# Linear attention feeding a swish MLP on one core: seven half products for batch 1 too, and a new order of loads, casts and sums around it

## The chip, the cores and the metric

The kernel runs on one core of a Trainium2 chip. The metric is the device time of one execution in microseconds (us); the time of a kernel is the median over its runs. Times inside an execution come from one profiled run and count from the start of its span.

The engines are TensorE (PE in the profile; its weight loads are PEld), VectorE (DVE), ScalarE (ACT), GpSimd (POOL) and SyncE (SP, which here only issues DMAs).

## The reference

Inputs q, k, v have the shape 8 x 8 x 576 x 64 (batch, heads, sequence, head size), float32. With phi(x) = max(x, 0) + 1 for positive x and exp(x) otherwise:

```python
kv  = einsum('bhsd,bhse->bhde', phi(k), v)
z   = sum over s of phi(k)
num = einsum('bhsd,bhde->bhse', phi(q), kv)
den = einsum('bhsd,bhd->bhs', phi(q), z)[..., None] + 1e-06
x   = (num / den), heads side by side: 4608 tokens x 512
h   = x @ w_in                      # 512 x 2048
g   = h / (1 + exp(-beta * h))
out = g @ w_out                     # 2048 x 512, output 4608 x 512
```

## The kernel before

**Tiling.** A batch has 576 tokens: 512 of them are handled in the batch's own stages, and the last 64 of every batch are collected in `xT_tail` and handled together as a ninth piece of 512. Matmuls take bfloat16 and sum in float32 in PSUM. TensorE's program is therefore H0, Y0, H1, Y1, ..., H8, Y8. Hb computes h for 16 blocks of 128 hidden units (`h_phase`, four matmuls of 512 columns a block, L401) and ScalarE turns each block into g by a SiLU (L409). Yb multiplies g with w_out. Batch 0 has code of its own; the loop at the end of the kernel runs b = 1 to 8.

**Work for later batches lies between.** During Hb, `side` lists (`sh`, run after a given block; `sy`, run after a given product of Yb) insert: `kv_both(b+1)` (72 small matmuls, L223, and a copy to `kv_q`), `numer_all(b+1)` (72 small matmuls, L333; VectorE then divides and writes `xs_sb`, the evacuation, L346 to L348; SP transposes it into xT, L355, and its last 64 tokens into `xT_tail`, four transposes, L368), and during Yb the phi of batch b+2: per half an exponential on ScalarE (L163), a ReLU (L168) and a minimum (L175) on VectorE, and for q two DMA transposes to `qTd` (L273), which the numerators read.

**Loads.** `next_loads(b+1)` stands on GpSimd after block 0 of Hb: two casts of v (float32 `vf` to bfloat16 `vaug`, L241), a copy into `gate` (L856) that waits for `qTd` of b+1 and so holds back what follows, and then the loads of q, k and v of batch b+2, in this order, on GpSimd's queue.

**Two forms of Y.** `y_phase` (b = 1) takes 4 token tiles times 16 blocks of g, 64 matmuls of 512 columns (L416); VectorE copies each tile out. `y_fast` (b = 2 to 8, the tuple FAST) computes a 2 x 2 block product by seven half-size products (L792), 16 matmuls of 256 columns each: pa, pd, pa again, pc, pb, pd again, pb again. Four of its operands are sums of parts of g (`gs`, 8 x 256 a partition each, written by `g_diff` after blocks 3 and 7 and by `g_sums` after blocks 11 and 15 of Hb, L722 to L728), four are sums of parts of w_out (`ws`, L710, two in H1 after block 15, two in H2 after blocks 7 and 8). Between the products VectorE adds: u2 = pc + r1 and u3 = pd + u2 (L816, L817), then y parts from pb + u3 (L827), pd + u2 (L830), pb + u2 (L838). The second pd product needs u3 read from its bank first, the last pb product needs the add at L827.

**Order.** Every engine runs its own instructions in the order in which the code issues them (`manual_schedule`); waits are on semaphores. PSUM banks rotate among four single banks (`bank`) and two double ones (`banks`).

Of the kernel before, what the change touches and what calls it, by code (L numbers as in the profile page):

```python
# [9 lines left out]
BF16 = mybir.dt.bfloat16  # L10
# [6 lines left out]
def kernel(  # L17
# [21 lines left out]
    EA = D + 1  # L39
    HM = DM // 2  # L40
    TINY = 2.0 ** -30
    FAST = tuple(range(2, 9))

    ctx.enter_context(tc.manual_schedule())

# [21 lines left out]
    w_in_sb = [consts.tile([P, KC, 512], BF16, name=f"w_in{i}") for i in range(4)]  # L67
    w_out_sb = [consts.tile([P, 4, DM], BF16, name=f"w_out{i}") for i in range(4)]

    xT = [consts.tile([P, 2, 4, 2, P], BF16, name=f"xT{i}") for i in range(2)]  # L70
    xT_tail = consts.tile([P, KC, B * G], BF16, name="xT_tail")
    g_sb = [consts.tile([P, FC, 512], BF16, name=f"g{i}") for i in range(2)]
    stage = consts.tile([P, 4096], F32, name="stage")
    warm = consts.tile([P, 512], BF16, name="warm")
# [21 lines left out]
    ws = [consts.tile([P, 8, HM], BF16, name=f"ws{i}") for i in range(4)] if FAST else None  # L96


    def load(eng, dst, src, b, i0=0, n=4):
# [109 lines left out]
    def half(hh):  # L209
        return slice(hh * G, (hh + 1) * G)  # L210
# [108 lines left out]
    def numer_all(b):  # L319

        h = [bank("nps"), bank("nps")]
        w = [banks("nps") for _ in range(2)]
        for v in (*range(7, 14), *range(7), *range(14, 18)):
            t, a = v // 4, v % 2
            for il in range(2):
                ps = h[il] if v // 7 == 1 else w[v // 14][:, il]  # L330
                for n in range(2):
                    pr, j = (v % 4 // 2, 2 * t + n) if v < 16 else (n, J - 1)
                    nc.tensor.matmul(  # L333
                        ps[half(n), v % 7 * EA : (v % 7 + 1) * EA],
                        st[b, "qTd"][half(il), a, pr * J + j, :],
                        kv_q[b % 2][half(il), a, pr, :],
                        start=True, stop=True, skip_group_check=True,
                    )
# [13 lines left out]

        def trans(t):
            for il in range(2):
                nc.sync.dma_start_transpose(  # L355
                    out=xT[b % 2][:, il, t : t + 2].rearrange("p t r n -> p (t r) n"),
                    in_=xs_sb[:, il, t * 4 * D : (t + 2) * 4 * D],
                )

        for il in range(2):  # L360
            evac(h[il][:, None], slice(il, il + 1), 7, 14)
        evac(w[0], slice(0, 2), 0, 7)
        trans(0)
        evac(w[1], slice(0, 2), 14, 18)
        trans(2)
        for pr in range(2):
            for il in range(2):
                nc.sync.dma_start_transpose(  # L368
                    out=xT_tail[:, 2 * pr + il, b * G : (b + 1) * G],
                    in_=xs_sb[half(pr), il, 16 * D : 18 * D],  # L370
                )

    def x_dst(b, t):
        if t < NT - 1:
            return xT[b % 2][:, :, t].rearrange("p i r n -> p r i n")
        return xT_tail[:, :, b * G : (b + 1) * G].rearrange("p (r i) n -> p r i n", i=2)

    def x_trans(b, t, eng, tp=None):
        n = rows_of(t)
# [7 lines left out]
        copy(eng, x_dst(b, t), tp[:, :, :n].rearrange("p (r i) n -> p r i n", i=2))  # L387

    def x_trans_dma(b, t=NT - 1):
        nc.sync.dma_start_transpose(  # L390
            out=xT_tail[:, :, b * G : (b + 1) * G], in_=st[b, "xs", t][: rows_of(t)]
        )


    def h_mm(x, ff, hp, c0=0, c1=512):
        for kc in range(KC):
            if x is xT_tail:
                xm = x[:, kc, c0:c1].rearrange("p (t n) -> p t n", n=P)
            else:
                xm = x[:, kc % 2, c0 // P : c1 // P, kc // 2]  # L400
            nc.tensor.matmul(  # L401
                hp[:, c0:c1].rearrange("p (t n) -> p t n", n=P),
                w_in_sb[ff // 4][:, kc, (ff % 4) * P : (ff % 4 + 1) * P],
                xm,
                start=(kc == 0), stop=(kc == KC - 1), skip_group_check=True,
            )
# [55 lines left out]
    def load_v(b):  # L462
        if b < B:
            load(nc.gpsimd, vf, v, b)


    idle(11)
# [162 lines left out]
    for x in ("q", "k"):  # L630
        phi_tile(1, x)
        for pr in range(2):
            phi_exp(1, x, pr, xin(1, x, pr))
            phi_relu(1, x, pr, xin(1, x, pr))
    phi_min(1, "q", 0)
    phi_min(1, "q", 1)
    for i in range(2):
# [55 lines left out]
        y_store(0, t)  # L693
    phi_all(2, "k", exps=False)

    if FAST:

        def wq(i, c0):
            return w_out_sb[i][:, :, c0 : c0 + HM]

        def w_sum(k, n):

            r = slice(4 * n, 4 * n + 4)
            a, b = (
                (wq(n, HM), wq(n, 0)),
                (wq(2 + n, HM), ws[0][:, r]),
                (wq(2 + n, HM), wq(n, HM)),
                (wq(2 + n, 0), ws[1][:, r]),
            )[k]
            nc.vector.tensor_sub(ws[k][:, r], a, b)  # L710


    def run(side, n):
        for f in side.get(n, ()):
# [9 lines left out]
    def g_sums(b, c0, c1):  # L724
# [2 lines left out]
        nc.vector.tensor_sub(gs[1][:, c], gs[0][:, c], g[:, c, 0:HM])  # L727
        nc.vector.tensor_sub(gs[3][:, c], g[:, c2, 0:HM], gs[1][:, c])  # L728

    def h_phase(b, x, side):  # L730
        for ff in range(FC):
            if b == 1 and ff in (4, 5):

                if ff == 4:
                    pair = banks("h_ps")
                    for i in range(2):
                        h_mm(x, ff + i, pair[:, i])
                hp = pair[:, ff - 4]
            else:
                hp = bank("h_ps")  # L740
                h_mm(x, ff, hp)
            silu(b, ff, hp)
# [7 lines left out]
    def y_phase(b, side):  # L750
        last = b == B
        for t in range(4):
            yp = bank("y_ps")
            if last and t == 3:
                for c0, c1 in ((0, 320), (320, 512)):
                    for i in range(4):
                        y_mm(b, t, i, yp, c0, c1)
                    y_out(b, t, yp, c0, c1)
                break
            for i in range(4):  # L760
                y_mm(b, t, i, yp)
                if i < 3:
                    run(side, 4 * t + i)
            y_out(b, t, yp)
            run(side, 4 * t + 3)

    def y_fast(b, side):

# [17 lines left out]
        def wsum(n):  # L786
            return lambda c: ws[n][:, c, :]

        def product(ps, lhs, rhs, first, ts=range(2), apart=False):
            for p in ts:  # L790
                for c in range(8):
                    nc.tensor.matmul(  # L792
                        ps[:, p * HM : (p + 1) * HM], lhs(c, p), rhs(c),
                        start=(first and (p == 0 or apart) and c == 0), stop=True,
# [21 lines left out]
        nc.vector.tensor_add(u2, pc, r1)  # L816
        nc.vector.tensor_add(u3, pd, u2)  # L817
        run(side, 3)
# [31 lines left out]

    def next_loads(b):

        for pr in range(2):
            v_copy(nc.gpsimd, b, pr)
        if b + 1 < B:
            nc.gpsimd.tensor_copy(gate, st[b, "qTd"][:, 1, 2 * J - 1, G - 1 : G])  # L856
            load_qk(b + 1)
            load_v(b + 1)

    for b in range(1, B + 1):  # L860
        n, m = b + 1, b + 2
# [5 lines left out]
        if b in (1, 2) and FAST:  # L867
            for k_ in ((0, 2), (1, 3))[b - 1]:
                for n_ in range(2):
                    at(sh, 15 if b == 1 else 7 + k_ // 2, lambda k_=k_, n_=n_: w_sum(k_, n_))  # L870
        if m < B:
            y = (lambda a, f: f) if b in FAST else (lambda a, f: a)
            at(sy, 0, lambda: phi_tile(m, "q"), lambda: phi_part(m, "q", 0))
            at(sy, 1, lambda: phi_part(m, "q", 1))
            at(sy, 1, lambda: q_trans_dma(m))
            at(sy, y(6, 3), lambda: phi_tile(m, "k"), lambda: phi_part(m, "k", 0))
            at(sy, y(8, 4), lambda: phi_part(m, "k", 1), lambda: table(ACTF.Silu))
        h_phase(b, xT[b % 2] if b < B else xT_tail, sh)
        (y_fast if b in FAST else y_phase)(b, sy)


# [28 lines left out]
```

## Time and profile before

| | us |
|---|---|
| median of 3 runs | 278.6 |
| lowest and highest | 277.94 and 280.63 |
| the profiled execution | 279.42 |
| its span, first to last instruction | 277.6 |
| TensorE's chain, H1 begins, Y1 begins, H2 begins | 51.5, 67.03, 80.84 |
| Y2 begins, H3 begins, Y3 begins | 96.70, 110.66, 126.35 |
| loads of batch 3 issued on GpSimd: q, k, v | 62.05, 62.78, 63.52 |
| their times from issue to landing | 6.9, 9.3, 12.4 |
| loads of batch 4 issued: q, k, v | 87.02, 87.76, 88.49 |
| their times from issue to landing | 6.7, 12.8, 16.6 |

A timeline line gives the start, the busy time, the engine, the line of the kernel, the operation, the tiles (written <- read), the type, how many instructions are merged, and in brackets the idle time before it and what ended that. A window line gives, for a stretch of the span, the length and each engine's busy time. Lines of the waits give who waited for whom, the total, how often and the longest.

Where the change does its work, SP's queue reads in the old kernel as follows: four transposes of x, four of its last tokens, then q's two, and the stores of y behind them.

```profile
91.12 10.01 SPq L355 DMA_TRANSPOSE xT<-xs_sb  x4
101.18 7.08 SPq L368 DMA_TRANSPOSE xT_tail<-xs_sb  x4
108.42 3.45 SPq L273 DMA_TRANSPOSE qTd<-phi_q  x2
111.97 2.06 SPq L834 DMA_DIRECT2D out_dram<-y  x2
```

### The profile page before, as it was taken

The page shows a single profiled execution, that of the slowest core. Times are in us where ns is not written, and L with a number is a line of the kernel's source. Part 1 is how long each engine was busy: PE and PEld are TensorE (multiplying, and loading weights), DVE is VectorE, ACT ScalarE, POOL GpSimd, SP SyncE. Part 2 cuts the span into 40 slices and gives each one's busy share as a digit, 9 for nine tenths or more (in the row PEclk, how much of TensorE's full clock was granted, in tenths as well). Part 3 has the DMA queues.
Part 4 walks back from the last instruction along what each step waited for, and adds up shares of the span by engine and source line. Part 5 has one row for each costly group of instructions (what it writes and reads, how often), then busy time and mean ns, then how long its engine had stood idle before and what let it go on. Part 6 is the DMA issues. An engine that isn't in the chain of part 4 may idle for free.

```text
span 277.6 us, 6371 instructions
## 1 busy us (share of the span) xinstructions
PE 269.1 (97%) x2697; PEld 167.5 (60%) x2697; DVE 163.4 (59%) x311; ACT 170.1 (61%) x232; POOL 44.3 (16%) x60
## 2 busy tenths in 40 slices
PE   7899999999999997999999999999999999999994
PEld 2585455444444486548854885488548844874584
DVE  4861485967946869467746784679464413341432
ACT  5738897965915793578557855785573077217610
POOL 5922011042033003300330033030000000000000
PEclk9979999999999999999999999999999999999999
DMA  7999999569938994899789979985621050023013
GB/s 253 239 206 353 269 372 267 140 106 186 278 69 144 232 207 75 195 175 227 89 165 233 211 73 185 259 159 68 176 57 31 0 153 0 0 48 105 0 40 113
DMA packets 49612, 42.76 MB, mean 154 GB/s; under 512 B 31136, under 2 KB 41392, under 8 KB 49584
## 3 DMA queue, kind: packets, MB, share of 16 engines
q0 software_dynamic: 13040, 23.40, 36.9%
q1 hardware_dynamic: 36368, 18.82, 35.8%
q8 instruction: 21, 0.34, 0.6%
q10 hardware_dynamic: 176, 0.14, 0.2%
q14 instruction: 7, 0.06, 0.1%
HBM read 36.71 MB, written 9.44 MB: 166 GB/s over the span
## 4 chain that ended last, share of the span: by engine, by line
PE 66%; SPq 4%; DVE 2%; DMA 2%; issue 1%; DVEq 0%
PE h_ps L401 34%; PE ya L792 9%; PE yb L792 8%; PE yd L792 8%; PE yc L792 4%; SPq L368 2%; DMA qTd<-phi_q 2%; PE nps L333 1%; PE kvp L223 1%; SPq L355 1%; DVE r L168 1%; SPq L273 0%; DVE ws L710 0%; DVE u L816 0%; DVE u L817 0%
## 5 line engine op out<-in xcount | busy, mean ns | idle before, releaser
L409 ACT ACTIVATE g<-h_ps,beta_c 128x512 bf16<-128x512 f32 x144 | 97.7, 688 | 70.5 <-PE h_ps L401 70.5
L401 PE MATMUL h_ps<-xT,w_in 128*128 128x512 bf16 (+1 forms) x560 | 114.5, 361 | 0.0
L401 PEld LDWEIGHTS <-w_in 128*128 128x128 bf16 x624 | 57.3, 98 | 62.3
L792 PEld LDWEIGHTS <-stage 128*128 128x128 bf16 x448 | 43.8, 98 | 7.0 <-issue 1.7
L792 PEld LDWEIGHTS <-g 128*128 128x128 bf16 x336 | 32.8, 98 | 5.4
L241 POOL CAST vaug<-vf 128x1152 bf16<-128x1152 f32 x13 | 16.8, 1319 | 82.1 <-DMA vf<-in_v_dram 82.1
L416 PE MATMUL y_ps<-w_out,g 128*128 128x512 bf16 x128 | 29.1, 379 | 0.0
L792 PE MATMUL ya<-w_out,g 128*128 128x256 bf16 x224 | 26.7, 273 | 0.0
L722 DVE TENSOR_TENSOR stage<-g 128x1024 bf16<-128x1024 bf16 x14 | 9.6, 689 | 22.9 <-ACT g L409 22.9
L726 DVE TENSOR_TENSOR stage<-g 128x1024 bf16<-128x1024 bf16 x14 | 9.7, 691 | 22.6 <-ACT g L409 22.6
L416 PEld LDWEIGHTS <-g 128*128 128x128 bf16 x128 | 12.2, 98 | 13.5
L348 DVE TENSOR_TENSOR xs_sb<-nps,rden 128x448 bf16<-128x448 f32 (+2 forms) x24 | 18.2, 758 | 0.8
L163 ACT ACTIVATE e<-xk 128x1152 bf16<-128x1152 bf16 (+1 forms) x15 | 16.7, 1159 | 0.2 <-DMA xk<-in_k_dram 0.2
L163 ACT ACTIVATE e<-xq 128x1152 bf16<-128x1152 bf16 x14 | 15.6, 1159 | 0.0
L175 DVE TENSOR_TENSOR phi_k<-e,r 128x1152 bf16<-128x1152 bf16 x16 | 14.3, 897 | 1.7 <-DVE r L168 0.5
L175 DVE TENSOR_TENSOR phi_q<-e,r 128x1152 bf16<-128x1152 bf16 x16 | 13.0, 814 | 3.6 <-ACT e L163 2.7
L792 PE MATMUL yb<-w_out,stage 128*128 128x256 bf16 x112 | 13.4, 272 | 1.6 <-DVE y L827 1.6
L156 ACT ACT_TABLE_LOAD x11 | 14.1, 1283 | 0.2
L401 PE MATMUL h_ps<-xT_tail,w_in 128*128 128x512 bf16 x64 | 14.0, 379 | 0.0
L816 DVE TENSOR_TENSOR u<-yc,r 128x512 f32<-128x512 f32 x7 | 4.8, 690 | 15.4 <-PE yc L792 15.4
L792 PE MATMUL yb<-ws,stage 128*128 128x256 bf16 x112 | 13.4, 273 | 0.0
L792 PE MATMUL yc<-ws,stage 128*128 128x256 bf16 x112 | 13.4, 273 | 0.0
(98 smaller groups left out, 238.7 us busy)
## 6 DMA issues: line engine op xcount, KB each, us to landing
vf<-in_v_dram POOLq DMA_DIRECT2D x7, 1152.0 KB, 15.1
out_dram<-y SPq DMA_DIRECT2D x25, 256.0 KB, 3.8
xq<-in_q_dram POOLq DMA_DIRECT2D x7, 576.0 KB, 8.7
xk<-in_k_dram POOLq DMA_DIRECT2D x7, 576.0 KB, 12.8
out_dram<-y SPq DMA_DIRECT2D x17, 128.0 KB, 3.3
w_in<-in_moe_w_in_dram POOLq DMA_DIRECT2D x4, 512.0 KB, 11.3
g<-in_moe_w_out_dram POOLq DMA_DIRECT2D x2, 1024.0 KB, 17.1
stage<-in_moe_w_out_dram POOLq DMA_DIRECT2D x2, 1024.0 KB, 21.8
```

Source lines behind the costliest of these rows:

```text
L156: nc.scalar.activation(act0, warm[:, 0:1], func)
L163: nc.scalar.activation(e, x, ACTF.Exp)
L175: nc.vector.tensor_tensor(st[b, a][:, pr].rearrange("p j (h d) -> p j h d", h=2), st[b, a, pr, "e"].rearrange("p h j d -> p j h d"), st[b, ...
L241: eng.tensor_copy(dst, src)
L348: nc.vector.tensor_mul(xs_sb[:, ils, v0 * D : v1 * D].rearrange("p i (u d) -> p i u d", d=D), pv[:, :, :, 0:D], rden[:, :, :, None].to_bro ...
L368: nc.sync.dma_start_transpose(out=xT_tail[:, 2 * pr + il, b * G : (b + 1) * G], in_=xs_sb[half(pr), il, 16 * D : 18 * D],)
L401: nc.tensor.matmul(hp[:, c0:c1].rearrange("p (t n) -> p t n", n=P), w_in_sb[ff // 4][:, kc, (ff % 4) * P : (ff % 4 + 1) * P], xm, start=(k ...
L409: nc.scalar.activation(g_sb[b % 2][:, ff, :], hp, ACTF.Silu, scale=beta_c[:, ff : ff + 1])
L416: nc.tensor.matmul(yp[:, c0:c1], g_sb[b % 2][:, ff, t * P : (t + 1) * P], w_out_sb[i][:, c, c0:c1], start=(ff == 0), stop=(ff == FC - 1), ...
L722: nc.vector.tensor_sub(gs[2][:, c], g[:, c, 0:HM], g[:, c, HM:512])
L726: nc.vector.tensor_add(gs[0][:, c], g[:, c, HM:512], g[:, c2, HM:512])
L792: nc.tensor.matmul(ps[:, p * HM : (p + 1) * HM], lhs(c, p), rhs(c), start=(first and (p == 0 or apart) and c == 0), stop=True, skip_group_ ...
```

## The change

It has four parts.

1. FAST and `y_phase` go; `y_fast` serves batch 1 too. The w sums move: `w_sum(0)` into Y0 (between q's and k's ReLUs of batch 1), `w_sum(2)` after block 4 and `w_sum(1)` after block 9 of H1, `w_sum(3)` after the first product of Y1. In Y1 the product pc takes four blocks of g for both token halves and then the other four.
2. In H1, what stands in the side list of a block comes ahead of that block's g sums, and batch 2's numerators stand after block 11 in place of 12. In H2 kv stands after block 2 and the numerators after block 5 (before: 1 and 4). In Y1, phi of batch 3 is spread: q's two exponentials early, q's ReLU and minimum after the adds of u3 and after the next y add, k's after the next two.
3. `next_loads` loads v first, then q and k, and the two casts of v stand behind these loads, that is in Hb after landing. (Batch 2's casts stay ahead of the gate.)
4. The last x transposes take the odd 64 tokens along as a fifth block (`trans(8, 18)`), and the four tail transposes of a batch go; GpSimd copies the fifth block from xT to `xT_tail` (`tail_copy`, after block 0 of Hb, ahead of the gate, for b = 2 to 7). `xT` and `xT_tail` get other layouts for it. Batch 1's tail is transposed in two pieces in place of one.

```diff
-    FAST = tuple(range(2, 9))
...
-    xT = [consts.tile([P, 2, 4, 2, P], BF16, name=f"xT{i}") for i in range(2)]
-    xT_tail = consts.tile([P, KC, B * G], BF16, name="xT_tail")
+    xT = [consts.tile([P, 2, 9, P], BF16, name=f"xT{i}") for i in range(2)]
+    xT_tail = consts.tile([P, 2, B, 2, G], BF16, name="xT_tail")
...
-        trans(0)
+        trans(0, 8)
         evac(w[1], slice(0, 2), 14, 18)
-        trans(2)
-        for pr in range(2):
-            for il in range(2):
-                nc.sync.dma_start_transpose(
-                    out=xT_tail[:, 2 * pr + il, b * G : (b + 1) * G],
-                    in_=xs_sb[half(pr), il, 16 * D : 18 * D],
-                )
+        trans(8, 18)
+
+    def tail_copy(b):
+        nc.gpsimd.tensor_copy(
+            xT_tail[:, :, b].rearrange("p i r n -> p i (r n)"), xT[b % 2][:, :, 8]
+        )
...
+        if x == "q":
+            w_sum(0)
...
             silu(b, ff, hp)
-            if b in FAST:
-                if ff in (3, 7):
-                    g_diff(b, slice(ff - 3, ff + 1))
-                if ff in (11, 15):
-                    g_sums(b, ff - 11, ff - 7)
+            if b > 1:
+                g_parts(b, ff)
             run(side, ff)
+            if b == 1:
+                g_parts(b, ff)
...
-        product(pc, sums(1), wsum(1), True)
+        product(pc, sums(1), wsum(1), True, step=4 if b == 1 else 8)
...
-        for pr in range(2):
+        for pr in range(2) if b == 2 else ():
             v_copy(nc.gpsimd, b, pr)
         if b + 1 < B:
             nc.gpsimd.tensor_copy(gate, st[b, "qTd"][:, 1, 2 * J - 1, G - 1 : G])
+            load_v(b + 1)
             load_qk(b + 1)
-            load_v(b + 1)
+            for pr in range(2):
+                v_copy(nc.gpsimd, b + 1, pr)
...
+        if 2 <= b < B:
+            at(sh, 0, lambda: tail_copy(b))
         if n < B:
             at(sh, 0, lambda: next_loads(n))
-            at(sh, 9 if b == 1 else 1, lambda: kv_both(n))
-            at(sh, 12 if b == 1 else 4, lambda: numer_all(n))
+            at(sh, {1: 9, 2: 2}.get(b, 1), lambda: kv_both(n))
+            at(sh, {1: 11, 2: 5}.get(b, 4), lambda: numer_all(n))
+        if b == 1:
+            at(sh, 4, lambda: w_sum(2))
+            at(sh, 9, lambda: w_sum(1))
+            at(sy, 0, lambda: w_sum(3))
         if m < B:
...
+            at(sy, 0, lambda: phi_tile(m, "q"), lambda: phi_tile(m, "k"))
+            if b == 1:
+                for pr in range(2):
+                    at(sy, 0, lambda pr=pr: phi_exp(m, "q", pr, xin(m, "q", pr)))
+                    at(sy, 3 + pr, lambda pr=pr: phi_relu(m, "q", pr, xin(m, "q", pr)))
+                    at(sy, 3 + pr, lambda pr=pr: phi_min(m, "q", pr))
+                at(sy, 4, lambda: q_trans_dma(m))
+                at(sy, 5, lambda: phi_part(m, "k", 0))
+                at(sy, 6, lambda: phi_part(m, "k", 1), lambda: table(ACTF.Silu))
+            else:
...
-        (y_fast if b in FAST else y_phase)(b, sy)
+        y_fast(b, sy)
```

For b = 2 to 5 the phi steps stay after products 0, 1, 3 and 4, as in the old kernel.

More of the change, by code (lines that the diff above doesn't have):

```diff
@@ L95 @@
     ]
-    ws = [consts.tile([P, 8, HM], BF16, name=f"ws{i}") for i in range(4)] if FAST else None
+    ws = [consts.tile([P, 8, HM], BF16, name=f"ws{i}") for i in range(4)]
     def load(eng, dst, src, b, i0=0, n=4):
@@ L351, in evac, with trans @@
             )
-        def trans(t):
+        def trans(v0, v1):
             for il in range(2):
                 nc.sync.dma_start_transpose(
-                    out=xT[b % 2][:, il, t : t + 2].rearrange("p t r n -> p (t r) n"),
-                    in_=xs_sb[:, il, t * 4 * D : (t + 2) * 4 * D],
+                    out=xT[b % 2][:, il, v0 // 2 : v1 // 2],
+                    in_=xs_sb[:, il, v0 * D : v1 * D],
                 )
@@ L362, in numer_all @@
         evac(w[0], slice(0, 2), 0, 7)
-        trans(0)
+        trans(0, 8)
         evac(w[1], slice(0, 2), 14, 18)
-        trans(2)
-        for pr in range(2):
-            for il in range(2):
-                nc.sync.dma_start_transpose(
-                    out=xT_tail[:, 2 * pr + il, b * G : (b + 1) * G],
-                    in_=xs_sb[half(pr), il, 16 * D : 18 * D],
-                )
+        trans(8, 18)
[3 more added lines that the diff above has]
+        )
     def x_dst(b, t):
         if t < NT - 1:
-            return xT[b % 2][:, :, t].rearrange("p i r n -> p r i n")
-        return xT_tail[:, :, b * G : (b + 1) * G].rearrange("p (r i) n -> p r i n", i=2)
+            return xT[b % 2][:, :, 2 * t : 2 * t + 2].rearrange("p i r n -> p r i n")
+        return xT_tail[:, :, b].rearrange("p i r n -> p r i n")
     def x_trans(b, t, eng, tp=None):
@@ L389, in x_trans_dma @@
     def x_trans_dma(b, t=NT - 1):
-        nc.sync.dma_start_transpose(
-            out=xT_tail[:, :, b * G : (b + 1) * G], in_=st[b, "xs", t][: rows_of(t)]
-        )
+        for pr in range(2):
+            nc.sync.dma_start_transpose(
+                out=xT_tail[:, :, b, pr],
+                in_=st[b, "xs", t][: rows_of(t), pr * HM : (pr + 1) * HM],
+            )
     def h_mm(x, ff, hp, c0=0, c1=512):
@@ L397, in h_mm @@
             if x is xT_tail:
-                xm = x[:, kc, c0:c1].rearrange("p (t n) -> p t n", n=P)
+                n, xm = G, x[:, kc % 2, :, kc // 2]
             else:
-                xm = x[:, kc % 2, c0 // P : c1 // P, kc // 2]
+                n, xm = P, x[:, kc % 2, 2 * (c0 // P) + kc // 2 : 2 * (c1 // P) : 2]
             nc.tensor.matmul(
-                hp[:, c0:c1].rearrange("p (t n) -> p t n", n=P),
+                hp[:, c0:c1].rearrange("p (t n) -> p t n", n=n),
                 w_in_sb[ff // 4][:, kc, (ff % 4) * P : (ff % 4 + 1) * P],
@@ L464, in load_v, with wq, w_sum @@
             load(nc.gpsimd, vf, v, b)
+    def wq(i, c0):
+        return w_out_sb[i][:, :, c0 : c0 + HM]
+    def w_sum(k):
+        for n in range(2):
+            r = slice(4 * n, 4 * n + 4)
+            a, b = (
+                (wq(n, HM), wq(n, 0)),
+                (wq(2 + n, HM), ws[0][:, r]),
+                (wq(2 + n, HM), wq(n, HM)),
+                (wq(2 + n, 0), ws[1][:, r]),
+            )[k]
+            nc.vector.tensor_sub(ws[k][:, r], a, b)
     idle(11)
@@ L694 @@
     phi_all(2, "k", exps=False)
[L696 to L710, printed above, removed]
     def run(side, n):
@@ L728, in g_sums, with g_parts @@
         nc.vector.tensor_sub(gs[3][:, c], g[:, c2, 0:HM], gs[1][:, c])
+    def g_parts(b, ff):
+        if ff in (3, 7):
+            g_diff(b, slice(ff - 3, ff + 1))
+        if ff in (11, 15):
+            g_sums(b, ff - 11, ff - 7)
     def h_phase(b, x, side):
@@ L742, in h_phase @@
             silu(b, ff, hp)
-            if b in FAST:
-                if ff in (3, 7):
-                    g_diff(b, slice(ff - 3, ff + 1))
-                if ff in (11, 15):
-                    g_sums(b, ff - 11, ff - 7)
-            run(side, ff)
[L750 to L765, printed above, removed]
+            if b > 1:
+                g_parts(b, ff)
+            run(side, ff)
+            if b == 1:
+                g_parts(b, ff)
     def y_fast(b, side):
@@ L787, in wsum, with product @@
             return lambda c: ws[n][:, c, :]
-        def product(ps, lhs, rhs, first, ts=range(2), apart=False):
-            for p in ts:
-                for c in range(8):
+        def product(ps, lhs, rhs, first, ts=range(2), apart=False, step=8):
+            for c0, p in [(c0, p) for c0 in range(0, 8, step) for p in ts]:
+                for c in range(c0, c0 + step):
                     nc.tensor.matmul(
@@ L862 @@
         sh, sy = {}, {}
+        if 2 <= b < B:
+            at(sh, 0, lambda: tail_copy(b))
         if n < B:
             at(sh, 0, lambda: next_loads(n))
-            at(sh, 9 if b == 1 else 1, lambda: kv_both(n))
-            at(sh, 12 if b == 1 else 4, lambda: numer_all(n))
[L867 to L870, printed above, removed]
-        if m < B:
[L872 to L877, printed above, removed]
+            at(sh, {1: 9, 2: 2}.get(b, 1), lambda: kv_both(n))
[4 more added lines that the diff above has]
+            at(sy, 0, lambda: w_sum(3))
+        if m < B:
+            at(sy, 0, lambda: phi_tile(m, "q"), lambda: phi_tile(m, "k"))
+            if b == 1:
+                for pr in range(2):
+                    at(sy, 0, lambda pr=pr: phi_exp(m, "q", pr, xin(m, "q", pr)))
[5 more added lines that the diff above has]
+            else:
+                at(sy, 0, lambda: phi_part(m, "q", 0))
+                at(sy, 1, lambda: phi_part(m, "q", 1))
+                at(sy, 1, lambda: q_trans_dma(m))
+                at(sy, 3, lambda: phi_part(m, "k", 0))
+                at(sy, 4, lambda: phi_part(m, "k", 1), lambda: table(ACTF.Silu))
         h_phase(b, xT[b % 2] if b < B else xT_tail, sh)
-        (y_fast if b in FAST else y_phase)(b, sy)
+        y_fast(b, sy)
 _INS = ['q', 'k', 'v', 'moe_w_in', 'moe_w_out', 'moe_beta']
```

## The prediction

> **What bounds the kernel now.** I read the page's busy table and clock row first, then the windows of the stages H1 (h of batch 1), Y1, H2, Y2, Y3, then TensorE's timeline with its waits, and last VectorE beside GpSimd wherever GpSimd casts v.
>
> ```profile
> PE 269.1 (97%) x2697; PEld 167.5 (60%) x2697; DVE 163.4 (59%) x311; ACT 170.1 (61%) x232; POOL 44.3 (16%) x60
> ...
> PEclk9979999999999999999999999999999999999999
> ```
>
> TensorE is busy 269.1 of 277.6 us at nearly full clock. Every piece below is therefore a number of TensorE instructions, or one of TensorE's waits. The windows are the five stages around the change (us, then PE, PEld, DVE, ACT, POOL busy, clock, DMA share, GB/s):
>
> ```profile
> 51.50:67.03 15.53, 15.53 (x210) 7.50 (x209) 10.71 (x23) 11.53 (x18) 5.02 (x7) 1.00 0.72 130
> 67.03:80.84 13.81, 13.81 (x65) 6.26 (x64) 11.04 (x19) 7.81 (x9) 3.04 (x2) 1.00 0.89 193
> 80.84:96.70 15.86, 15.60 (x210) 7.51 (x208) 11.07 (x23) 10.29 (x15) 2.54 (x4) 1.00 0.96 175
> 96.70:110.66 13.96, 12.39 (x113) 10.95 (x112) 10.50 (x15) 8.97 (x12) 2.46 (x2) 1.00 0.91 143
> ...
> 126.35:138.58 12.23, 12.23 (x113) 10.88 (x112) 9.17 (x15) 8.95 (x11) 2.24 (x2) 1.00 0.96 142
> ```
>
> Y1 with whole products takes 13.81 us; Y3, with seven half products, 12.23. Y2 has the same products as Y3 and takes 13.96. TensorE's waits explain the rest; after 52 us it has only these two:
>
> ```profile
> PE yb L792 <- DVE y L827: 1.6, 1, 1.6
> PE nps L333 <- DMA qTd<-phi_q: 0.3, 1, 0.3
> ```
>
> Why Y2 waits is seen on VectorE (first five lines) against GpSimd's cast of v (sixth). A ReLU that takes 0.45 elsewhere takes 1.43 here, and a minimum 1.50 instead of 0.76, so the add that frees bank yb is late:
>
> ```profile
> 103.89 0.69 DVE L816 TENSOR_TENSOR u<-yc,r 128x512 f32<-128x512 f32 x1 [1.22 <-PE yc L792]
> 104.61 0.69 DVE L817 TENSOR_TENSOR u<-yd,u 128x512 f32<-128x512 f32 x1
> 105.22 1.43 DVE L168 TENSOR_SCALAR r<-xk 128x1152 bf16<-128x1152 bf16 x1
> 106.76 1.50 DVE L175 TENSOR_TENSOR phi_k<-e,r 128x1152 bf16<-128x1152 bf16 x1
> 108.19 0.68 DVE L827 TENSOR_TENSOR y<-yb,u 128x512 f32<-128x512 f32 x1
> ```
> ```profile
> 105.19 2.46 POOL L241 CAST vaug<-vf 128x1152 bf16<-128x1152 f32 x2 [15.92 <-DMA vf<-in_v_dram]
> ```
>
> So the most that the change can give is Y1's saving plus these two waits. What it may cost is new waits of TensorE in Y1, H2 and Y2, where VectorE gets more work.
>
> **Y1 by seven products.** 64 matmuls of 512 columns (13.81 us) become 112 of 256 columns. Y3's chain has 16 of them every 1.75 us, seven times 12.23. TensorE: -1.6 us by these windows, and -1.75 by Y1's own row of 64 matmuls (13.98, with the fill); I take -1.6. ScalarE gains two copies (0.57 and 0.58), beside idle time: it stands 5.76 us before H2.
>
> **VectorE in H1 and Y1.** Four copies of y (0.68) become five adds (0.69). New in H1: two g differences (0.69), two groups of three g sums (one every 0.72), and w_sum(2), w_sum(1) (1.21 a pair), with w_sum(3) in Y1. w_sum(0) goes into Y0 between the ReLUs of q and k, where VectorE stands 2.05 us for k's load: nothing, as 1.21 fits; if k came earlier, at most 1.21 on a VectorE that has 1.74 more idle before kv_bd.
>
> I walk the new order from 59.5, where phi_k of batch 2 ends in the old trace. Difference 60.2, w_sum(2) 61.4, difference 62.1, kv copy (0.43) 62.5, w_sum(1) 63.7. TensorE wants the numerators, now after block 11, at 62.7: cover 0.2 us. Evacuation takes 4.45 us (64.13 to 68.58 now): 68.2. g sums 72.5, w_sum(3) 73.7. TensorE wants the sums for product yc at 67.03+5.24 = 72.3 and, as yc takes them by halves, the second half at 73.15; it is ready at 71.8. Then u2, u3 (1.42) from yc's end 74.0 to 75.45, wanted by yd at 75.77; q's first ReLU and minimum (1.23) and the add (0.68) to 77.4, wanted at 77.5 by the last product. Undisturbed, Y1 just fits, with 0.1 to 0.3 us over at each step.
>
> **v first, cast in H.** The gate falls at 61.60 as before. What is loaded first lands 6.9 us after its issue at 62.05 (xq now), so v lands near 69 and its two casts follow at once, beside the g sums. No row shows a cast beside them in Y1, but there are three meetings of the two casts with VectorE on SBUF operands. They cost it 1.00 (casts at 55.27, a ReLU of 0.71 for 0.45 and a minimum of 1.50 for 0.76), 1.72 (Y2 above) and 1.89:
>
> ```profile
> 184.03 1.63 DVE L728 TENSOR_TENSOR stage<-g,stage 128x1024 bf16<-128x1024 bf16 x1
> 185.59 1.40 DVE L168 TENSOR_SCALAR r<-xq 128x1152 bf16<-128x1152 bf16 x1
> ```
>
> I take the mean, 1.54. w_sum(3) then ends at 75.2, u3 at 76.65, and yd starts 0.9 late; the last add is late by another 0.1. Y1's wait: +1.0. The bounds are 0 (casts during the evacuation, which reads PSUM; the L311 evacuation at 55.42 kept its 0.68 beside a cast) and +1.4 (1.89 instead of 1.54). The Trainium skill speaks against this move: "SBUF — State Buffer", section "SBUF: two separate sides", says that VectorE and GpSimd hold a shared port pair by an exclusive lock for a whole instruction, also against VectorE operations with two SBUF inputs. By that rule both casts would be lost in full, by the trace's 1.15 us each 2.3 in place of 1.54, and Y1 would wait 0.8 longer; the rows above show 1.0 to 1.9.
>
> **H2.** It would start at 67.03+12.23+1.0 = 80.25. Its kv comes a block later than now, at 82.85, its second half at 83.2. VectorE has, after the add at 78.5, q's second half 79.7, an add 80.4, k's first half 81.6, an add 82.3, k's second half 83.5: a wait of 0.3 (bounds 0 undisturbed, 0.7 at 1.89). q's transposes start at 79.7 and need 6.1 (80.28 to 86.39 now): 85.8, for numerators wanted at 86.5, so that wait of 0.26 goes. k's exponentials wait for the last load of the three, which lands now at 63.52+12.4 = 75.9; two of 1.15 and a table load of 1.28 end by 79.7, before the first silu. xT's last transpose lands now at 72.2+6.9 = 79.1; the numerators are 0.8 earlier but two transposes grow from 8 to 10 blocks: nothing here, 0 to 0.5 if H2 starts at 79.3. Together +0.3-0.26 = 0.0.
>
> **Y2.** The casts leave it, and 2.49 us of w sums leave H2's VectorE. v lands near 93.5, and the casts meet g's sums in H2, whose last gs[1] ends at 99.0 where 101.9 is soon enough: up to 1.89 is covered by 2.9. But k is now the last load. The last one landed at 88.49+16.6 = 105.1; exponential, minimum and add (1.15+0.69+0.68) give 107.6, where Y2 starting at 96.15 wants yb's add at 106.6. At 104.1 it costs nothing. The wait of 1.57 becomes 0 to 1.0; I take 0.3, as the four odd transposes that ran among these loads are gone: -1.27.
>
> **Odd x in the last transposes, tail copy, stores.** On SP's queue four odd transposes per batch go (5.0 to 7.1 us each set). q's transposes stand right behind them (108.42 in Y2, phi_q being ready at 102.7), so qTd, the gate and all loads of H3 to H5 come 4 to 6 us sooner. That pays for the 3.8 us that v takes ahead of q and k there. The tail copy on GpSimd (256 elements; about 0.3 from 1.15 per 1152) stands ahead of the gate, which waits 7 us there; xT has landed by then. Batch 1 has two tail transposes for one (2.0 more on SP): its y stores end at 67.0 for 65.0, and the xT transposes behind them want the queue near 67. No TensorE work is added. Cost: 0.
>
> **Sum.** -1.6+1.0+0.0-1.27 = -1.9: a span of 275.7, and 277.5 for the profiled execution (279.42, 1.8 over its span). That execution is 0.8 over the median of the runs, 278.6; against that the forecast is 276.7.
>
> **Rivals.** (A, 0.55) as summed, 275.9 (0.2 in Y1) to 277.6 (1.4 in Y1, 0.8 in Y2). (B, 0.27) clean: the casts miss the g sums, and both old waits go: -1.6-0.26-1.57 = -3.4, 275.2. For it: Y1 fits undisturbed and Y3 runs without a wait. Against it: covers of 0.1 to 0.3 us. (C, 0.13) given back: VectorE loses 1.89 in Y1 (+1.4), kv waits 0.7, xT 0.3, Y2 still waits 1.0: -1.6+1.4+0.7+0.3-0.26-0.57 = 0, 278.6. (D, 0.05) slower: q and k land too late behind v in every Y that has phi, Y1 to Y5. In Y3 the last load landed at 132.0 and k's exponential must begin by about 134.3; it decides when k lands over 2.3 us later than v does now. With 1.3 us in five stages, less B's 3.4, that is +3.1, 281.7. The gate's earlier time speaks against it.
>
> **Numbers.** 1% of 278.6 is 2.8 us, about what a measurement of this kernel tells from no change. Faster than 275.8: B, and 0.08 from A, whose lower end lies at that bound, 0.35 in all; slower: D, 0.05; within: 0.60. Range 275.0 to 278.4: B, A and most of C.
>
> **What would show it.** Right: Y1 near 13.2 us with one or two waits of TensorE on VectorE (yd behind u3), casts at 69 to 72 with g sums or w sums of about 1.6 for 0.69; Y2 without the casts at 12.2 to 13.2; gates from H3 on at the start of their H. Wrong: Y1 at 12.23 with casts outside the sums (B); TensorE waiting for xT, kv or ScalarE's k in H2 (C); ReLUs that wait for loads in Y3 to Y5 (D); any wait in H6 to Y8, where nothing changes.

## The result and the profile after

| | kernel before | changed kernel |
|---|---|---|
| median, us (22 runs each) | 278.13 | 277.16 |
| lowest and highest, us | 277.25 to 280.63 | 276.39 to 279.06 |
| ratio to before | | 0.996 (0.9942 to 0.9978) |
| profiled execution and its span, us | 279.42, 277.6 | 276.85, 275.1 |

The change saves 1.0 us by the medians, 0.6 to 1.6 by the interval of the ratio. The time lies in the predicted range (275.0 to 278.4) and 0.5 over the predicted 276.7. The two first profiled executions are 2.6 us apart, much more than the medians; the experiments show why. Part of the spread goes with the clock that TensorE was granted: the 13 timed executions of the changed kernel at a granted clock of 0.998 or more took 276.39 to 277.55 us, the two at 0.986 took 278.66 and 279.06.

The windows of the changed kernel (H1, Y1, H2, Y2, H3, Y3), in the columns of the prediction's windows:

```profile
51.27:66.80 15.53, 15.53 (x211) 7.52 (x210) 14.82 (x30) 11.53 (x18) 5.39 (x7) 1.00 0.61 144
66.80:79.93 13.13, 12.66 (x114) 10.86 (x112) 12.54 (x19) 7.43 (x10) 3.10 (x3) 1.00 1.13 187
79.93:95.59 15.66, 15.66 (x211) 7.55 (x208) 10.95 (x24) 11.67 (x18) 2.44 (x4) 1.00 0.89 200
95.59:108.00 12.41, 12.41 (x114) 10.95 (x113) 10.44 (x15) 9.06 (x12) 3.41 (x3) 1.00 1.06 162
108.00:123.52 15.52, 15.52 (x211) 7.51 (x209) 9.09 (x19) 10.29 (x15) 5.13 (x6) 1.00 0.99 223
123.52:135.75 12.23, 12.23 (x113) 10.95 (x112) 9.83 (x16) 8.97 (x12) 0.49 (x1) 1.00 0.76 104
```

Y1 went from 13.81 to 13.13, H2 from 15.86 to 15.66, Y2 from 13.96 to 12.41. VectorE is now busy 12.54 of Y1's 13.13 us (11.04 of 13.81 before). After the start the profile lists one wait of TensorE in the changed kernel:

```profile
PE yd L781 <- DVE u L806: 0.5, 1, 0.5
```

It is the wait for u3 ahead of the second yd product. VectorE's timeline in Y1 and GpSimd's casts show where it comes from:

```profile
69.17 0.69 DVE L729 TENSOR_TENSOR stage<-g,stage 128x1024 bf16<-128x1024 bf16 x1
69.78 1.63 DVE L727 TENSOR_TENSOR stage<-g 128x1024 bf16<-128x1024 bf16 x1
71.45 1.51 DVE L728 TENSOR_TENSOR stage<-stage,g 128x1024 bf16<-128x1024 bf16 x1
72.99 0.69 DVE L729 TENSOR_TENSOR stage<-g,stage 128x1024 bf16<-128x1024 bf16 x1
73.60 1.29 DVE L479 TENSOR_TENSOR ws<-w_out,ws 128x1024 bf16<-128x1024 bf16 x2
74.81 0.69 DVE L805 TENSOR_TENSOR u<-yc,r 128x512 f32<-128x512 f32 x1
75.53 0.69 DVE L806 TENSOR_TENSOR u<-yd,u 128x512 f32<-128x512 f32 x1
```
```profile
69.71 2.71 POOL L240 CAST vaug<-vf 128x1152 bf16<-128x1152 f32 x2 [5.68 <-DMA vf<-in_v_dram]
```

Two g sums take 1.63 and 1.51 us in place of 0.69 while GpSimd casts (69.71 to 72.42); that is 1.76 us of VectorE's time. u3 ends at 76.2, and TensorE, ready for yd at 75.8, waits.

### The profile page after: what moved, and what is told of

It reads as the page before. It is cut to its first block, busy times and chain, and to the rows that moved or that the text cites. A ratio compares the mean times of both kernels' runs of the same rounds, so it can differ in the third digit from the quotient of the medians.

```text
span 275.1 us, 6447 instructions
## 1 busy us (share of the span) xinstructions
PE 266.0 (97%) x2745; PEld 170.9 (62%) x2745; DVE 168.7 (61%) x320; ACT 171.1 (62%) x235; POOL 47.8 (17%) x66
## 4 chain that ended last, share of the span: by engine, by line
PE 83%; DVE 12%; DMA 2%; issue 1%; SPq 0%; ACT 0%; DVEq 0%
PE h_ps L401 41%; PE yb L781 10%; PE yd L781 10%; PE ya L781 9%; PE yc L781 4%; PE y_ps L416 4%; DMA stage<-in_k_dram 2%; PE kvp L222 2%; PE nps L332 1%; DVE r L167 1%; DVE ws L479 1%; DVE phi_k L174 1%; DVE xs_sb L347 1%; DVE y L240 1%; DVE stage L728 1%
## 5 line engine op out<-in xcount | busy, mean ns | idle before, releaser
L781 PEld LDWEIGHTS <-stage 128*128 128x128 bf16 x512 | 50.0, 98 | 6.3 <-DVE stage L728 0.2
L781 PEld LDWEIGHTS <-g 128*128 128x128 bf16 x384 | 37.5, 98 | 6.8 <-issue 0.6
L781 PE MATMUL ya<-w_out,g 128*128 128x256 bf16 x256 | 30.6, 273 | 0.0
L727 DVE TENSOR_TENSOR stage<-g 128x1024 bf16<-128x1024 bf16 x16 | 12.8, 802 | 23.0 <-ACT g L409 23.0
L723 DVE TENSOR_TENSOR stage<-g 128x1024 bf16<-128x1024 bf16 x16 | 11.0, 688 | 21.9 <-ACT g L409 21.9
L781 PE MATMUL yd<-ws,g 128*128 128x256 bf16 x128 | 15.3, 272 | 0.5 <-DVE u L806 0.5
L781 PE MATMUL yc<-ws,stage 128*128 128x256 bf16 x128 | 15.4, 273 | 0.0
L781 PE MATMUL yb<-ws,stage 128*128 128x256 bf16 x128 | 15.3, 273 | 0.0
L781 PE MATMUL yd<-ws,stage 128*128 128x256 bf16 x128 | 15.3, 273 | 0.0
L781 PE MATMUL yb<-w_out,stage 128*128 128x256 bf16 x128 | 15.3, 272 | 0.0
L416 PE MATMUL y_ps<-w_out,g 128*128 128x512 bf16 x64 | 15.1, 379 | 0.0
## 6 DMA issues: line engine op xcount, KB each, us to landing
xq<-in_q_dram POOLq DMA_DIRECT2D x7, 576.0 KB, 12.7
xk<-in_k_dram POOLq DMA_DIRECT2D x7, 576.0 KB, 15.5
```

What stands on the lines that cost most here:

```text
L416: nc.tensor.matmul(yp[:, c0:c1], g_sb[b % 2][:, ff, t * P : (t + 1) * P], w_out_sb[i][:, c, c0:c1], start=(ff == 0), stop=(ff == FC - 1), ...
L723: nc.vector.tensor_sub(gs[2][:, c], g[:, c, 0:HM], g[:, c, HM:512])
L727: nc.vector.tensor_add(gs[0][:, c], g[:, c, HM:512], g[:, c2, HM:512])
L781: nc.tensor.matmul(ps[:, p * HM : (p + 1) * HM], lhs(c, p), rhs(c), start=(first and (p == 0 or apart) and c == 0), stop=True, skip_group_ ...
```

## The experiments

Each kernel was timed beside the kernel before on the same chip: 12 executions each, 6 of old_loads and one of look_before. rep_before, rep_after, y1_whole and cast_act shared one chip (the kernel before took 277.77 there), look_before, cast_act_two, old_odd and old_loads a second (277.54), the other four a third (277.69). The ratio is the recorded one and not the quotient of two medians. "H1 to H3" is the stretch from the first matmul of H1 to the first of H3 in the run's own profiled execution, which leaves out the start-up, in which executions differ by up to 1.1 us.

| run | median, us | ratio (95%) | H1 to H3, us | Y1, H2, Y2, us |
|---|---|---|---|---|
| first profile of before | | | 59.16 | 13.81, 15.86, 13.96 |
| rep_before | 277.63 | 1.000 (0.997 to 1.003) | 57.30 | 13.81, 15.73, 12.23 |
| look_before | 277.25 | | 57.37 | 13.81, 15.53, 12.50 |
| first profile of the changed kernel | | | 56.73 | 13.13, 15.66, 12.41 |
| rep_after | 277.31 | 0.9979 (0.9954 to 1.0004) | 56.56 | 13.13, 15.66, 12.24 |
| rep_after2 | 277.30 | 0.9981 (0.9958 to 1.0004) | 56.66 | 13.12, 15.67, 12.34 |
| y1_whole | 277.91 | 0.9999 (0.9971 to 1.0026) | 57.10 | 13.81, 15.53, 12.23 |
| cast_act | 276.93 | 0.9956 (0.9923 to 0.9988) | 56.91 | 12.39, 15.85, 13.14 |
| cast_act_two | 276.49 | 0.9971 (0.9949 to 0.9994) | 55.83 | 12.39, 15.65, 12.29 |
| cast_act_two2 | 276.84 | 0.9961 (0.9938 to 0.9984) | 55.90 | 12.38, 15.73, 12.29 |
| old_odd | 276.82 | 0.9975 (0.9953 to 0.9996) | 56.54 | 13.12, 15.66, 12.23 |
| old_loads | 280.87 | 1.0105 (1.0065 to 1.0144) | 58.57 | 12.59, 16.89, 13.56 |
| tail_late | 277.99 | 1.000 (0.9976 to 1.0023) | 57.04 | 12.39, 16.89, 12.23 |
| old_both | 278.99 | 1.0036 (1.0011 to 1.0061) | 58.08 | 12.39, 16.95, 13.21 |

### The kernel before, twice more

> The kernel before, once more: a second profiled execution. In the first one TensorE waited 1.57 us in Y2 (for the add behind a ReLU and a minimum that met v's casts). Theory T1: this wait is the same in every execution, 1.4 to 1.7 again, Y2 13.9 to 14.0 us. Rival T2: it depends on when v of batch 4 lands, and the first profiled execution (279.42, 1.3 over the median of 22) was an unlucky one: the wait is under 0.8 here. T2 would explain why the medians differ by 1.0 and the two traces by 2.5.

> The kernel before, a third profiled execution. Y2 waited 1.57 us in the first and not at all in the second. If its wait is an accident of when v lands (casts beginning after 104 against 103), it lies between 0 and 1.6 again; nothing near 1.5 in each would have been expected of a fixed wait.

In both, the profile lists no wait of TensorE after H1 begins. Y2 of rep_before on VectorE, the same rows that the prediction showed of the first execution, and its casts:

```profile
103.95 0.69 DVE L816 TENSOR_TENSOR u<-yc,r 128x512 f32<-128x512 f32 x1 [1.22 <-PE yc L792]
104.67 0.69 DVE L817 TENSOR_TENSOR u<-yd,u 128x512 f32<-128x512 f32 x1
105.28 0.45 DVE L168 TENSOR_SCALAR r<-xk 128x1152 bf16<-128x1152 bf16 x1
105.83 0.76 DVE L175 TENSOR_TENSOR phi_k<-e,r 128x1152 bf16<-128x1152 bf16 x1
106.51 0.68 DVE L827 TENSOR_TENSOR y<-yb,u 128x512 f32<-128x512 f32 x1
```
```profile
102.98 2.24 POOL L241 CAST vaug<-vf 128x1152 bf16<-128x1152 f32 x2 [13.65 <-DMA vf<-in_v_dram]
```

v landed 14.3 us after its issue here, 16.6 in the first execution, so the casts began at 102.98 in place of 105.19. They fell into the time in which VectorE waited for yc and ran u2 and u3, two sums with one operand in PSUM, which kept their 0.69; the ReLU of k came behind them. In look_before (v after 14.7 us) they began at 102.54 and cost one ReLU 0.27, and Y2 took 12.50. T2 held: the wait of 1.57 that carried two thirds of the predicted gain belongs to one execution and is absent in the other two.

### The changed kernel, twice more

> The changed kernel, once more. T1 and T2 alike: Y1 13.0 to 13.3 us with one wait of 0.3 to 0.6 of TensorE for u3, Y2 12.3 to 12.6. If the wait in Y1 varies as v's landing does, it lies between 0 and 1.0. Ratio to the kernel before 0.994 to 0.998.

> The changed kernel, beside the others of this call: ratio 0.995 to 0.998; Y1 13.0 to 13.3 with a wait of 0.4 to 0.6 for u3, Y2 12.2 to 12.6.

Y1 took 13.13, 13.13 and 13.12 us in three executions, each with the wait of 0.46 for u3. The casts began, as v landed, at 70.07 and 69.32 here, 18.3 us after H1's start (18.4 in the first execution), and the two sums took 1.63 and 1.51 again: the meeting with the g sums is no accident.

The intervals of both ratios reach 1: here the whole kernel gained 0.4 to 0.5 us by the medians, against 1.0 in the first comparison. More of these executions ran under a granted clock of 0.998 (5 and 6 of 12) than of the kernel before beside them (8 and 9 of 35). Among those at 0.998 or more the medians are 276.71 (7) against 277.62 (27), and 276.80 (6) against 277.57 (26): 0.9 and 0.8 us less, a little more than Y1's 0.68. Of the 69 executions of the kernel before at that clock, on three chips, 14 took over 278.4 us and the slowest 280.76; of the changed kernel's 26, the 13 of the first comparison among them, none took over 277.55.

### Y1 by whole products

```diff
-            if b == 1:
-                g_parts(b, ff)
...
-        y_fast(b, sy)
+        (y_fast if b > 1 else y_phase)(b, sy)
```

With it the old `y_phase` comes back for batch 1, and phi of batch 3 stands after its pieces 0, 1, 6 and 8 as in the kernel before.

> The changed kernel with Y1 by 64 whole products again (no g sums in H1; the w sums stay where the change put them; phi of batch 3 between them). Theory: Y1 13.8 us, so 0.6 to 0.7 over the changed kernel's 13.13, and Y2 stays without a wait, as that came from the order of loads and transposes. Rival: the seven products are worth nothing net because of the new waits (same time); or Y2's wait returns, as it hangs on Y1's form.

Y1 is 13.81 again and Y2 has no wait. The seven products are worth 0.68 us in Y1, and 0.4 to 0.5 over H1 to H3, as H2 is 0.1 and Y2 up to 0.2 shorter here; by the medians on one chip 277.91 against 277.31, with intervals that overlap. So by the traces nearly all that the change gives is this part: with the other parts alone the time is that of the kernel before (0.9999). Y2 without a wait does not hang on Y1's form; that it came from the order of loads is not shown, as rep_before has none either.

### v's casts on ScalarE

```diff
-            for pr in range(2):
+            for pr in range(2) if b > 2 else ():
                 v_copy(nc.gpsimd, b + 1, pr)
...
+                for pr in range(2):
+                    at(sy, 0, lambda pr=pr: v_copy(nc.scalar, m, pr))
```

> The changed kernel with the two casts of v of batch 3 on ScalarE in Y1, where it stands 4.0 us for q, in place of GpSimd. Theory: the wait of 0.46 in Y1 and the 0.13 in H2's kv come from the casts that met the g sums (1.63 and 1.51 us for 0.69): both go, Y1 12.2 to 12.3 us, 0.5 to 0.6 us less than the changed kernel. Rival: VectorE's order in Y1 is too long by itself: the wait stays above 0.3. A third: v's casts hold up q's exponentials on ScalarE, and Y1 waits for q's ReLU and minimum instead.

In Y1 the theory held. Two VectorE rows of Y1 and ScalarE's casts:

```profile
69.44 0.69 DVE L727 TENSOR_TENSOR stage<-g 128x1024 bf16<-128x1024 bf16 x1
70.15 0.69 DVE L728 TENSOR_TENSOR stage<-stage,g 128x1024 bf16<-128x1024 bf16 x1
```
```profile
69.44 2.21 ACT L238 CAST vaug<-vf 128x1152 bf16<-128x1152 f32 x2
```

The same casts at the same time on ScalarE cost these sums nothing; the wait goes and Y1 takes 12.39. But this execution has a new wait of 0.67 in Y2, which the theory had not foreseen: H2 began earlier, and batch 4's loads, issued 1.1 us earlier, landed hardly earlier (q at 99.65 for 99.8). VectorE in Y2, and ScalarE's exponentials:

```profile
99.64 0.46 DVE L167 TENSOR_SCALAR r<-xq 128x1152 bf16<-128x1152 bf16 x1 [0.22 <-DMA xq<-in_q_dram]
100.89 0.76 DVE L174 TENSOR_TENSOR phi_q<-e,r 128x1152 bf16<-128x1152 bf16 x1 [0.80 <-ACT e L162]
...
102.80 0.68 DVE L805 TENSOR_TENSOR u<-yc,r 128x512 f32<-128x512 f32 x1
```
```profile
99.70 2.22 ACT L162 ACTIVATE e<-xq 128x1152 bf16<-128x1152 bf16 x2 [2.12 <-DMA xq<-in_q_dram]
```

VectorE waits for q's load and then for its exponential, with u2 queued behind. The timed executions do not show the gain of Y1 lost again, though: 276.93 against 277.31 on one chip, while this profiled execution is 0.35 longer from H1 to H3 than rep_after's. The next kernel also puts phi between Y2's sums, and v's casts of batch 4 on ScalarE:

```diff
-            for pr in range(2) if b > 2 else ():
+            for pr in range(2) if b > 3 else ():
                 v_copy(nc.gpsimd, b + 1, pr)
...
-            if b == 1:
+            if b in (1, 2):
+                for pr in range(2):
+                    at(sy, 0, lambda pr=pr: v_copy(nc.scalar, m, pr))
                 for pr in range(2):
                     at(sy, 0, lambda pr=pr: phi_exp(m, "q", pr, xin(m, "q", pr)))
...
-            at(sh, {1: 9, 2: 2}.get(b, 1), lambda: kv_both(n))
-            at(sh, {1: 11, 2: 5}.get(b, 4), lambda: numer_all(n))
+            at(sh, {1: 9, 2: 2, 3: 2}.get(b, 1), lambda: kv_both(n))
+            at(sh, {1: 11, 2: 5, 3: 5}.get(b, 4), lambda: numer_all(n))
```

> The changed kernel with v's casts of batches 3 and 4 both on ScalarE (Y1, Y2), and in Y2 phi put between the sums as in Y1 (kv and numerators of batch 4 a block later in H3). With the first alone, Y1 lost its wait and Y2 got one of 0.67, where q's load landed at 99.6 and its ReLU and minimum stood ahead of u2. Theory: that wait was q's load, and here it goes: Y1 12.2 to 12.4, Y2 12.2 to 12.5, 0.5 to 1.0 below the changed kernel. Rival: the loads are the bound by now, and the wait moves on into H3 (kv or numerators) or Y3.

> v's casts of batches 3 and 4 on ScalarE and phi between Y2's sums, once more, beside the changed kernel on the same chip. Theory: 0.6 to 1.0 us below the changed kernel (its H1-to-H3 stretch was 55.8 us against 56.6 and 56.7). Rival: equal medians, as other executions lose it again to late loads.

Both waits are gone; the windows of Y1 and Y2 in cast_act_two:

```profile
66.46:78.85 12.39, 12.39 (x114) 10.95 (x113) 10.87 (x19) 9.48 (x12) 0.38 (x1) 1.00 1.10 195
...
94.50:106.79 12.29, 12.29 (x114) 10.95 (x112) 6.88 (x12) 10.97 (x14) 0.40 (x1) 1.00 0.70 103
```

That the new order in Y2 removed the wait there is not shown. Here q's exponentials began at 99.38, right behind the casts on ScalarE, and waited for no load: q, issued at 85.86, landed after 11.0 us (11.3 in cast_act_two2), in cast_act, issued at 85.95, after 13.7. Up to that point both kernels issue the same instructions, so this is a difference between executions, or chips, and not of the edit. cast_act's wait may be of the same kind as the one in Y2 of the kernel before.

H1 to H3 is 0.7 to 0.9 us shorter than the changed kernel's. Beside it on the same chip the medians are 276.84 and 277.30: 0.46 less, under the 0.6 to 1.0 that was expected, but not equal. cast_act and both runs of this kernel are below the kernel before beyond their intervals (0.9956; 0.9971 and 0.9961), and at a granted clock of 0.998 or more their medians are 276.25 (6 executions), 276.24 and 276.31 (9 each). So the casts of batch 3 on ScalarE are worth about 0.4 to 0.5 us; that the second step adds anything the timed executions do not show.

### The other two parts undone

The four tail transposes again, without the tail copy:

```diff
-        trans(8, 18)
+        trans(8, 16)
+        for pr in range(2):
+            for il in range(2):
+                nc.sync.dma_start_transpose(
+                    out=xT_tail[:, il, b, pr],
+                    in_=xs_sb[half(pr), il, 16 * D : 18 * D],
+                )
...
-        if 2 <= b < B:
-            at(sh, 0, lambda: tail_copy(b))
```

> The changed kernel with four tail transposes per batch again and no tail copy. Theory: SP's queue holds q's transposes back by 3 to 6 us in Y1, so that the numerators in H2 wait 1 to 3 us for qTd, and gates from H3 on come 4 us later; the time rises by 1 to 3 us. Rival: q's transposes still land in time (within 0.3).

The rival held: no wait for qTd, the same windows, and a ratio of 0.9975 against 0.9979 and 0.9981. SP's queue in Y1 and Y2:

```profile
73.54 5.48 SPq L367 DMA_TRANSPOSE xT_tail<-xs_sb  x4
79.21 3.46 SPq L272 DMA_TRANSPOSE qTd<-phi_q  x2
...
98.47 5.04 SPq L367 DMA_TRANSPOSE xT_tail<-xs_sb  x4
103.68 3.49 SPq L272 DMA_TRANSPOSE qTd<-phi_q  x2
```

The four end at 79.0 and 103.5, and q's transposes follow at 79.21 and 103.68; in the changed kernel, with nothing ahead of them, these start at 79.51 and 103.19. The theory's 1 to 3 us did not come: this part is worth nothing that these runs can tell.

Three more kernels go back to the old load order, with the casts again ahead of the next gate (old_loads, below). tail_late also moves the tail copy behind the next loads; old_both also has the old tail transposes and no tail copy:

```diff
-        for pr in range(2) if b == 2 else ():
+        for pr in range(2):
             v_copy(nc.gpsimd, b, pr)
...
-            load_v(b + 1)
             load_qk(b + 1)
-            for pr in range(2):
-                v_copy(nc.gpsimd, b + 1, pr)
+            load_v(b + 1)
```

> The changed kernel with the loads in the old order (q, k, v) and the casts of v again ahead of the next gate. Theory: v of batch 3 then lands near 76 and its casts leave the g sums of Y1 (0.69 each again), so that yd no longer waits for u3; they come among q's and k's ReLUs and minima instead, where each may cost VectorE 0.7 to 1.0, and the last add of Y1 or kv in H2 waits 0.5 to 1.5. Y2 keeps its wait only if v of batch 4 lands after its start plus 7 us. Sum against the changed kernel: 0 to +1. Rival: the order of loads is worth nothing either way (within 0.3).

> The changed kernel with the loads in the old order, as in old_loads, but the tail copy behind the next loads in place of ahead of the casts. In old_loads (ratio 1.0105) v of batch 3 had landed by about 76, but its casts began at 81.4, right behind a tail copy that had waited for xT until 80.6; kv waited 1.0 and Y2 and Y5 waited 1.2 and 1.3 for casts beside phi. Theory: the copy held the casts; here they begin near 75 to 76 in Y1 and near 103 in Y2, and the time comes down to 277 to 278.5 (ratio 0.998 to 1.003); Y1 may wait up to 1.5 for its last add. Rival: the old load order itself costs the 3 us, and the time stays above 280.

> Loads, casts and odd transposes as in the kernel before; of the change only Y1's seven products and the order in H1, Y1, H2 are left. Theory: the seven products alone are worth what the whole change is, less what v's casts near 76 cost Y1 (0.5 to 1.5): time within 0.5 us of the kernel before. Rival: without the tail copy nothing holds the casts and it equals the changed kernel, 0.996 to 0.998. As in tail_late the casts begin near 76.

old_loads is 1% slower than the kernel before, more than expected. GpSimd's rows show a cause that no theory had named:

```profile
80.62 0.83 POOL L367 COPY xT_tail<-xT 128x256 bf16<-128x256 bf16 x1 [15.89 <-DMA xT<-xs_sb]
81.40 2.46 POOL L240 CAST vaug<-vf 128x1152 bf16<-128x1152 f32 x2
```

The tail copy waits for xT and holds the casts behind it on its engine, until they meet k's phi. With the copy moved back (tail_late, on another chip) the time falls by 1.0%, to that of the kernel before: the theory held for the copy. The casts did not begin near 76, though, but at 78.10, as v landed later; then they hit q's second minimum, and kv in H2 waited 1.2. old_both, without any tail copy, does the same in Y1 and H2 (VectorE, then all of TensorE's waits after H1 begins):

```profile
78.23 1.70 DVE L174 TENSOR_TENSOR phi_q<-e,r 128x1152 bf16<-128x1152 bf16 x1
79.85 0.68 DVE L825 TENSOR_TENSOR y<-yd,u 128x512 f32<-128x512 f32 x1
80.45 0.80 DVE L167 TENSOR_SCALAR r<-xk 128x1152 bf16<-128x1152 bf16 x1
```
```profile
PE kvp L222 <- DVE phi_k L174: 1.2, 1, 1.2
PE yb L787 <- DVE y L822: 0.8, 1, 0.8
```

Its Y1 is 12.39, without a wait, but H2 takes 16.95: what Y1 gains, H2 and Y2 lose, and it is 0.4% slower than before (1.0036), not within the 0.5 us that was expected. So in these runs, with the casts on GpSimd, the seven products for batch 1 pay only with v loaded first. The old load order with the casts on ScalarE was not run.

## Why the prediction was right, and where it was off

**Bound by TensorE; Y1 -1.6 and +1.0.** Right in its mechanism, and in its total partly by luck. The casts began at 69.71 (69 predicted), met the second group of g sums, and cost VectorE 1.76 us (1.54 taken, bounds 1.0 to 1.9). u3 ended at 76.2 (76.65), as VectorE was half a microsecond ahead of the walk, and the wait listed is 0.46 where 0.9 was taken. Of the rest the sum has only 0.1, for the last add: yb starts 1.86 after yc, yd 2.37 after yb, the last product 1.91 after yd, where 1.75 is usual, 0.89 too much together, the wait included. So Y1 lost 0.9 to 12.23, where 1.0 was taken: Y1 is 13.13, and 13.2 was named. cast_act shows the cause of all but 0.16: with the same casts on ScalarE there is no wait and Y1 takes 12.39, with 1.91 ahead of the last product still. The lock that the Trainium skill states ("SBUF — State Buffer", section "SBUF: two separate sides") would have cost 2.3 us, an estimate by the trace's 1.15 per cast. The trace agrees with it in place and not in full: 1.76 was measured, 0.94 and 0.82 of 1.15.

**H2, 0.0.** Right within 0.2: kv took 0.94 for 0.81, the numerators did not wait, H2 is 15.66, where before it was 15.53 to 15.86 in three executions. The wait of 0.26 for qTd that the sum took away was absent in the two other executions of the kernel before.

**Y2, -1.27.** This step failed, in its starting point rather than its end. Y2 after is 12.24 to 12.41 us, and 12.5 was forecast. But the 13.96 before, taken from one profiled execution, was 12.23 and 12.50 in the two others. Against those Y2 after is between 0.3 us shorter and 0.2 longer. Without this term the sum is a gain of 0.6, where 1.9 was forecast; 1.0 was measured in the first comparison, 0.4 to 0.5 in the repeats. The casts did not leave Y2 either: v landed at 95.9 (93.5 forecast), they ran from 96.08 to 98.77, in Y2's first 3 us, and stretched two g sums to 1.26 and 1.51. That cost 1.39 of the 2.9 that the prediction found free there, and no wait.

**The sum.** The forecast set this gain, read from an execution 1.3 above the median 278.13 of all 22, against the 278.6 of the first three. The gain was 0.9 too large and the start 0.5 too high; the two errors offset each other in part, and that the time misses by only 0.5 is to that extent luck. The prediction took 1%, 2.8 us, as what a measurement tells from no change; the interval of the ratio was under 0.2% to each side.

**v first, cast in H.** Its price was seen, its worth was not. The runs show that without it the new Y1 gains nothing (old_both and tail_late), since v's casts on GpSimd come near 78 then and delay kv by 1.2.

**Odd x, 0 with "4 to 6 us sooner" for the loads from H3 on.** The cost of 0 held. The 4 to 6 us came from the same unlucky execution (q's transposes at 108.42); they start at 106.18 and 105.09 in the other two, and at 103.19 in the changed kernel. The sign named for it, gates at the start of their H from H3 on, came in H4 and H5 (0.1 and 0.6 us in), not in H3 (3.0). With the other parts of the change in place the tail transposes end in time anyway (old_odd).

**Rivals.** A was the case in Y1, by its mechanism, while the wait that it took out of Y2 is absent from two of three profiled executions; B did not come, as the g sums were hit in each of three executions; C's wait in kv was 0.13 in the changed kernel, where C took 0.7, but 1.2 in old_both, and D's late q is what one execution of cast_act met when Y1 was shortened further.

**What stays open.** How often the kernel before has Y2's wait: one of three profiled executions had it, and the timed runs have no trace. Their times at full granted clock allow it in about one of five (14 of 69 over 278.4 us) and none of the changed kernel's 26, so that the other three parts may take a tail away and not the median; no trace shows that this tail is Y2's wait. Whether the changed kernel is granted a lower clock more often: 20 of its 46 executions with a recorded clock were under 0.998, of the kernel before 24 of 93. And why a load, issued at the same time by the same instructions, lands after 6.9 us in one execution and 10.7 in another.

## What to carry to other kernels

A wait in a profile is first a fact of one execution: profile the old kernel again before its removal is counted as a gain, above all if the wait hangs on when a load lands. The same holds for a wait that an experiment shows for the first time. Walk the new instruction order of the second-busiest engine with the durations of the trace, and look at which other engine works on SBUF beside it at that time; here this named the place and nearly the size of Y1's loss beforehand. Try an engine that stands idle beside the crowded one (ScalarE, 4 us) for such a cast. A small copy that waits on a DMA must not stand ahead of urgent work on an engine that runs its instructions in order: here it cost 1%.

## What the runs showed of the hardware

Two casts of 128x1152 on GpSimd stretched bfloat16 sums of two SBUF operands from 0.69 to 1.63 and 1.51 us, in each of three executions of the changed kernel, and took 2.71 to 2.85 themselves in place of 2.24; on ScalarE the same casts took 2.21 and the sums 0.69. Sums with one operand in PSUM kept 0.69 beside such casts (u2 and u3 of rep_before, from 103.95 on).

Three loads issued one after the other on one queue landed by place, v first: 9.6, 12.7 and 15.5 us after their issue in H2 of the changed kernel, 7.8, 10.9 and 13.6 in y1_whole. The first of these figures does not carry over to another execution: v, issued at 85.20 and 85.11 by the same instructions, landed after 10.7 us in cast_act and 6.9 in cast_act_two.
